# Attention and two feed-forward layers in one kernel: the second phase as a list that the kernel orders itself, silu and gate in one ScalarE step, additions kept in PSUM

## The chip, the cores and the metric

The kernel runs on one core of one Trainium2 chip. The metric is the time of one execution on the device in microseconds (us). The kernel before takes 1124.02 us (median of 3 runs, 1121.6 to 1125.26).

## The reference

The inputs are 4 batches with 8 heads of 576 positions and a head dimension of 64, and 2304 tokens of width 512 go through two feed-forward layers.

```python
scores = scale * (q @ k.T)                      # causal
attn = softmax(scores + minimum(bias, 0))       # bias from cumsum(maximum(s, 0))
x = (attn @ v) as [2304, 512]

xn = x / sqrt(mean(x * x) + 1e-6) * rms_g       # layer 1
g = xn @ w_gate                                 # 512 x 1536
x = (g / (1 + exp(-g)) * (xn @ w_val)) @ w_out  # silu(g) * val, 1536 x 512

h = x @ w_in                                    # layer 2: 512 x 2048
out = (h / (1 + exp(-1.702 * h))) @ w_out       # gate function, 2048 x 512
```

All weights come as 64-bit floats, all else is float32.

## The kernel before, in words

**Number format.** TensorE works on rounded float32. To keep float32 accuracy every operand is split into a rounded part (hi) and the rest (lo), and each product is three matmuls: hi x hi, hi x lo, lo x hi. So behind every intermediate result stand two small steps: `rnd` (a copy on ScalarE, L97) writes hi, `rest` (`scalar_tensor_tensor` on VectorE, L112) writes lo.

**Weights.** They arrive as 64-bit words in units of 128 x 512 (512 KB) by SP's queue. `decode` (L132) makes float32 of one unit: a step on ScalarE (L144), VectorE (L145), GpSimd (L146), VectorE (L147, L149) and GpSimd (L151). The result is then split into hi and lo.

**First phase** (L175 to L627). The 32 heads of attention run one after the other as events with times of their own; the first four chunks (of 128 hidden units) of layer 1 for tokens 0 to 1727 run between them. At its end stand the mean square of the last batch (`rms_mean`, L470 to L480: a root by 12 small steps on 128 x 5 elements on VectorE) and the norm (`rms_apply`, L496).

**Second phase** (`phase_b`, L630). It computes the rest of layer 1 and all of layer 2. The tokens form three blocks p = 0, 1, 2 of 768, each seen as two halves of 384. A list `jobs` (L761) gives the sequence: job P (chunk 4 on block 0), two jobs R (the four first chunks for the remaining 576 tokens, 288 each), ten jobs of layer 1 with chunks 5 to 11 and the rest of 4, twelve jobs of layer 2. A job of the last two kinds has one to three groups and then its outputs.

A *group* (`start_group` L871, `group` L878) is a fast 2 x 2 block product: seven products instead of eight, each of 6 matmuls of 384 columns (`mul`, L858). On the side of the tokens it needs seven *pieces* of the block's input (B11, T1, T2, B22, T3, B21, T4; `MAKE`, L800), each 128 x 2 x 2 x 384 hi and lo, 768 KB; on the side of the weights quarter blocks and four sums of them (S1 to S4, in `front`). There are 23 groups in layer 1 and 24 in layer 2. Its steps off TensorE: three copies out of PSUM on ScalarE (into B, m5 and v1), two additions on VectorE (L889, L896), then `hidden` (L839): tanh on ScalarE (L842) into SBUF and `(tanh + 1) * x` on VectorE (L843); in layer 1 `times` (L854) multiplies this by the other half (L855); then `split_h` (L848) makes hi and lo. That is two hidden blocks in a group of layer 1, four in layer 2.

The *outputs* of a job (`down_part`, L913) are matmuls from the hidden blocks: 384 columns in layer 1 (L922), 512 in layer 2 (L919), 288 in job R; `evac` (L925) adds them to `xT` in SBUF or copies them out.

**Buffers.** PSUM has eight banks: A 2, B 2, E 1, y 3 (L638 to L641). Seven rotating tiles `pc` hold the pieces in use. Two tiles `mk` serve to make pieces *ahead*: while other jobs run, the three blocks' pieces are cut into `mk` and stored in DRAM (`put`, L787, called by way of `pieces`, L803), and at a change of job each of the seven pieces is loaded when the last group of the old job has read its own (`load_piece`, L821).

**What sets the order.** The framework's scheduler places every instruction by priority, which follows the order of the program text; the text itself interleaves the work of later jobs by tables: how many weight units a job decodes (`WPLAN`, L769) and how many pieces it makes ahead (`XSEQ`, `XPLAN`, L771), spread over a job by the class `Spread` (L971). Each engine then executes its queue strictly in that order.

```python
XSEQ = [("1", 2), ("1", 0), ("2", 2), ("2", 1), ("2", 0)]
XPLAN = {2: 3, 3: 4, 5: 7, 11: 4, 12: 5, 13: 5, 14: 7}
...
th = ew.tile([P, H2], F32, tag="th", name="th", bufs=PRM["THB"])[:, :n]
nc.scalar.activation(out=th, in_=src, func=AF.Tanh, scale=0.5 if up is not None else 0.851)
nc.vector.scalar_tensor_tensor(out=th, in0=th, scalar=1.0, in1=src, op0=ALU.add, op1=ALU.mult)
```

## Time and profile before

| | |
|---|---|
| median of 3 runs | 1124.02 us (1121.6 to 1125.26) |
| profiled execution | 1132.93 us |
| its span | 1131.1 us |
| instructions | 17737 |
| mean granted TensorE clock, of full speed | 0.968 |
| HBM read, written | 145.06 MB, 44.26 MB |
| second phase on TensorE | 363.9 to 1127.3 us |

Busy time counts an engine's compute instructions; issuing a transfer or waiting is not in it. "PE" is TensorE's matmuls, "PEld" its weight loads, which run beside them. The span is divided below into stages of the second phase: 363.9 to 395 us (job P and the end of the norm), 395 to 440 (jobs R), 440 to 500 (first groups of layer 1), 500 to 640, 640 to 800 (the change of layers lies in it), and 800 to the end (layer 2). The granted clock is a share of full speed. In a row of idle time, the name behind "<-" is what the engine waited for last.

### The profile page before, as it was taken

What the parts mean: (1) busy time and instruction counts of PE and PEld (TensorE: products, weight loads), DVE (VectorE), ACT (ScalarE), POOL (GpSimd) and SP (SyncE); (2) the same over time, 40 slices, a digit from 0 to 9 for tenths busy, and PEclk for the clock granted to TensorE, in tenths of its full rate; (3) what the DMA queues carried; (4) which work ended last, traced back from release to release, by engine and by line L of the source; (5) the groups of instructions that cost most, each with busy time, mean ns of one, the idle gap of its engine ahead of it and who ended that gap; (6) DMA issues with size and microseconds to landing.
All of it is one profiled execution on the core that took longest, in us unless ns stands there. A gap on an engine that the chain in (4) does not pass through costs nothing.

```text
span 1131.1 us, 17737 instructions
## 1 busy us (share of the span) xinstructions
PE 1057.9 (94%) x6200; PEld 982.0 (87%) x6200; DVE 785.6 (69%) x1625; ACT 574.0 (51%) x1338; POOL 572.0 (51%) x608
## 2 busy tenths in 40 slices
PE   7998999998999698699999999888999999999998
PEld 5776898998999698598999999887888899898987
DVE  6668678678766878585775687986567587556443
ACT  5675677678555445334433445455555344333331
POOL 6788768377832756453640565663265166042000
PEclk9998899999899898798999999999999999999999
DMA  5445424144102477945274258978946516522651
GB/s 151 125 128 141 131 75 125 56 119 124 34 20 75 152 276 276 388 188 218 84 242 164 70 184 327 326 288 308 325 160 221 205 57 217 207 98 70 214 209 66
DMA packets 64511, 193.58 MB, mean 171 GB/s; under 512 B 7091, under 2 KB 26035, under 8 KB 64422
## 3 DMA queue, kind: packets, MB, share of 16 engines
q1 hardware_dynamic: 64310, 192.37, 49.6%
q8 instruction: 49, 0.80, 0.3%
q14 instruction: 40, 0.33, 0.1%
q10 hardware_dynamic: 112, 0.08, 0.0%
HBM read 145.06 MB, written 44.26 MB: 167 GB/s over the span
## 4 chain that ended last, share of the span: by engine, by line
PE 42%; DVE 6%; DMA 5%; ACT 2%; issue 2%; POOL 2%; POOLq 0%; DVEq 0%; ACTq 0%
PE y L919 15%; PE B L863 9%; PE y L922 6%; PE A L863 6%; PE E L863 6%; DMA wst<-in_w_dram 2%; DVE th L843 1%; DVE hh L112 1%; DMA pc<-pc21T 1%; POOL wa L151 1%; DMA pc22B<-mk 1%; ACT th L842 1%; DMA pc<-pc11T 1%; DVE wm L145 1%; DVE wa L149 1%
## 5 line engine op out<-in xcount | busy, mean ns | idle before, releaser
L919 PE MATMUL y<-wu,hh 128*128 128x512 f32 x864 | 213.5, 393 | 6.3 <-ACT hh L97 2.7
L919 PEld LDWEIGHTS y<-wu,hh 128*128 128x128 f32 x864 | 160.4, 188 | 38.9 <-ACT hh L97 4.7
L863 PE MATMUL B<-pc,wu 128*128 128x384 f32 x846 | 172.7, 339 | 6.3 <-ACT th L842 2.8
L863 PEld LDWEIGHTS B<-pc,wu 128*128 128x128 f32 x846 | 151.6, 191 | 10.1 <-ACT th L842 3.1
L112 DVE SCALAR_TENSOR_TENSOR hh<-th,hh 128x384 fp32r<-128x384 f32 (+3 forms) x180 | 128.2, 725 | 39.2 <-ACT hh L97 37.4
L863 PE MATMUL A<-pc,wu 128*128 128x384 f32 x600 | 130.8, 345 | 16.2 <-DVE th L843 13.7
L922 PE MATMUL y<-hh,wu 128*128 128x384 f32 (+1 forms) x672 | 128.1, 331 | 2.3 <-DVE hh L112 1.2
L863 PEld LDWEIGHTS A<-pc,wu 128*128 128x128 f32 x600 | 109.6, 194 | 21.5 <-DVE th L843 15.3
L863 PE MATMUL E<-pc,wu 128*128 128x384 f32 x576 | 121.6, 342 | 4.9 <-DVE xT L496 2.6
L97 ACT ACTIVATE hh<-th 128x384 fp32r<-128x384 f32 (+3 forms) x173 | 84.9, 502 | 69.3 <-DVE th L855 39.1
L922 PEld LDWEIGHTS y<-hh,wu 128*128 128x128 f32 x672 | 115.6, 190 | 3.5 <-DVE hh L112 1.5
L151 POOL TENSOR_TENSOR wa<-wa,wst 128x512 int32<-128x512 int32 x52 | 74.2, 1426 | 77.3 <-DVE wa L149 73.5
L863 PEld LDWEIGHTS E<-pc,wu 128*128 128x128 f32 x576 | 104.8, 193 | 7.3 <-issue 2.9
L687 POOL TENSOR_TENSOR wu<-wa,wu 128x512 fp32r<-128x512 f32 x39 | 54.9, 1408 | 98.9 <-ACT wu L97 98.7
L362 POOL TENSOR_SCALAR p<-p,RC 128x64 f32<-128x64 f32 (+4 forms) x160 | 90.4, 585 | 24.9 <-DVE RC L350 19.5
L166 PE MATMUL gv<-x,wu 128*128 128x256 f32 (+1 forms) x672 | 98.5, 294 | 0.9 <-DVE xT L496 0.9
L338 ACT ACTIVATE p<-p,MX 128x64 f32<-128x64 f32 (+4 forms) x160 | 88.4, 555 | 21.0 <-DVE MX L328 20.5
L166 PEld LDWEIGHTS gv<-x,wu 128*128 128x128 f32 x672 | 90.3, 199 | 1.7 <-issue 1.1
L144 ACT ACTIVATE wst<-wst 128x512 int32<-128x512 uint32 x68 | 46.0, 677 | 86.4 <-DMA wst<-in_w_dram 84.8
L328 DVE CUSTOM_DVE_ANT_0 p<-s,mask 128x64 f32<-128x64 f32 (+4 forms) x160 | 64.7, 422 | 23.8 <-PE s L315 10.9
L382 PE MATMUL t<-ident,p 128*128 128x128 f32 x448 | 74.8, 279 | 4.2 <-ACT pt L103 3.4
L146 POOL TENSOR_SCALAR wm<-wm 128x512 f32<-128x512 f32 x68 | 48.1, 707 | 48.7 <-DVE wm L145 47.5
(141 smaller groups left out, 2076.0 us busy)
## 6 DMA issues: line engine op xcount, KB each, us to landing
wst<-in_w_dram SPq DMA_DIRECT2D x68, 512.0 KB
pc<-pc21T SPq DMA_DIRECT2D x16, 768.0 KB
pc<-pc22T SPq DMA_DIRECT2D x12, 768.0 KB
pc<-pc21B SPq DMA_DIRECT2D x12, 768.0 KB
QS<-in_qT_dram SPq DMA_DIRECT2D x53, 144.0 KB
KS<-in_kT_dram SPq DMA_DIRECT2D x53, 144.0 KB
pc<-pc22B SPq DMA_DIRECT2D x9, 768.0 KB
pc<-pc12T SPq DMA_DIRECT2D x8, 768.0 KB
```

The lines of the kernel that those rows point to most:

```text
L97: nc.scalar.activation(out=o, in_=i, func=AF.Copy, scale=c)
L112: eng.scalar_tensor_tensor(out=o, in0=i, scalar=c, in1=hi, op0=ALU.mult, op1=ALU.subtract)
L151: nc.gpsimd.tensor_tensor(out=ai, in0=ai, in1=li, op=ALU.add)
L166: nc.tensor.matmul(o, w[:, a, wc:wc + P], x(b, k), start=first and n == 0, stop=last and n == 2,)
L328: nc.vector.tensor_tensor_reduce(out=pt[:m, k0:k0 + n], in0=ps[:m, c0:c0 + n], in1=mask[:m, moff:moff + n], scale=-0.125, scalar=mx[:, 4:5 ...
L338: nc.scalar.activation(out=d["p", qb][:m, :], in_=d["p", qb][:m, :], func=AF.Exp, scale=-1.0, bias=MXt[h % NB][:m, col:col + 1], accum_out ...
L362: eng.tensor_scalar(out=pt[:m, :], in0=pt[:m, :], scalar1=RCt[h % NB][:m, qb:qb + 1], scalar2=1.0, op0=ALU.mult, op1=ALU.mult,)
L382: nc.tensor.transpose(ps[:, c:c + m], d["p", qb][:, Q0[kb]:Q0[kb] + P], ident)
L687: lo.tensor_tensor(out=dst[:, 1, :n], in0=src, in1=dst[:, 0, :n], op=ALU.subtract)
L863: nc.tensor.matmul(o[:, :H2], u[:, a, off + k * P:off + k * P + P], pc[:, b, k, :], start=first and k == 0 and m == 0, stop=fin and k == 1 ...
L919: nc.tensor.matmul(ps, hh[c, t][:, a, q * P:q * P + P], wu[layer, c, "o"][:, b, :], start=st, stop=sp_)
L922: nc.tensor.matmul(ps[:, :n], wu["1", c, "o"][:, a, q * P:q * P + P], hh[c, t][:, b, :n], start=st, stop=sp_)
```

## The change

**One list.** `phase_b` no longer issues instructions. Each step is recorded by `op` (L691 of the new kernel) with its engine, its length in us, and the names that it reads and writes; a step marked "VG" may run on VectorE or GpSimd. From the names the dependences follow. A list scheduler then goes through time with these lengths: it keeps an earliest and a latest start of each step, lets VectorE and GpSimd exclude each other in steps marked `port`, models one DMA queue, gives each engine, of what can run, the step with the earliest latest start, and holds an engine back for a short while if a more urgent step is about to be ready. TensorE's own order is that of the text. The result is fixed by dependences between neighbours on each engine. Steps whose start falls before `ET` = 6 us of the phase are issued with priorities among the last events of the first phase; `close_heads` gives back some of that phase's buffers earlier for it.

**Activation.** Silu in layer 1 and the gate function in layer 2 are one ScalarE instruction each (`AF.Silu`, `AF.Gelu_apprx_sigmoid`) in place of tanh, addition and product. In layer 1 it writes `SG` in SBUF, and the product with the other half is written back to PSUM; in layer 2 it works in place. The additions of the group's products are in PSUM too (m5 in layer 2 excepted), and hi and lo are cut from there by a copy and a subtraction.

**Buffers.** Each piece has one fixed tile, six PSUM banks (`FB`) are given out in turn, and two (`BB`) belong to the groups alternately.

**Pieces.** Nothing is made ahead. At a change of job `piece` loads a piece that is in DRAM, or makes it in its tile from `xT` and stores it. The first three products of the next job stand among the last group and the outputs of the old one.

Diff, cut to its core:

```diff
-        XSEQ = [("1", 2), ("1", 0), ("2", 2), ("2", 1), ("2", 0)]
-        XPLAN = {2: 3, 3: 4, 5: 7, 11: 4, 12: 5, 13: 5, 14: 7}
...
-            th = ew.tile([P, H2], F32, tag="th", name="th", bufs=PRM["THB"])[:, :n]
-            nc.scalar.activation(out=th, in_=src, func=AF.Tanh, scale=0.5 if up is not None else 0.851)
-            nc.vector.scalar_tensor_tensor(out=th, in0=th, scalar=1.0, in1=src, op0=ALU.add, op1=ALU.mult)
...
+    def close_heads():
+        pr.close()
+        fs["br"] = ctx.enter_context(tc.tile_pool(name="br", bufs=1, side="right", reuse_waits="tile"))
...
+        def sub(o_, x, y, n, r, w):
+            op("VG", (0.04 + n * 0.00118, 0.1 + n * 0.0025),
+               lambda e: e.tensor_tensor(out=o_, in0=x, in1=y, op=ALU.subtract), r, w, port=True)
+
+        def cp(o_, i_, cost, r, w, t0=-99.0):
+            op("A", cost, lambda e: e.activation(out=o_, in_=i_, func=AF.Copy, scale=1.0), r, w, t0=t0)
...
+        def piece(layer, p, nm):
+
+            key = (layer, p, nm)
+            if key in made:
+                dma(flat(PC[nm]), pc_d[key], 6 << 17, [("pd",) + key], [("pc", nm), ("pc", nm, "lo")])
+                return
+            made.add(key)
+            o, ab = next((o, ab) for x, o, ab in MAKE if x == nm)
+            k, t = BL[o]
+            if ab:
+                (ka, ta), (kb, tb) = BL[ab[0]], BL[ab[1]]
+                sub(xv(k, p, t), xv(ka, p, ta), xv(kb, p, tb), 2 * H2, [xk(ka, p, ta), xk(kb, p, tb)], [xk(k, p, t)])
+            cut(PC[nm], ("pc", nm), xv(k, p, t), xk(k, p, t))
+            dma(pc_d[key], flat(PC[nm]), 6 << 17, [("pc", nm), ("pc", nm, "lo")], [("pd",) + key])
...
+        def split_h(key, src, sk, n, psum):
+            s = new_hh()
+            t = HH[s]
+            cp(t[:, 0, :n], src, 0.17 + n * 0.0008 if psum else 0.53, [sk], [("hh", s)])
+            if psum:
+                op("V", 0.03 + n * 0.00136, lambda e: e.tensor_tensor(out=t[:, 1, :n], in0=src, in1=t[:, 0, :n], op=ALU.subtract),
+                   [sk, ("hh", s)], [("hh", s, "lo")])
...
+        def act(o_, i_, func, n, r, w):
+            op("A", 0.17 + n * 0.0008, lambda e: e.activation(out=o_, in_=i_, func=func), r, w)
+
+        def add(o_, x, y, n, r, w, o=ALU.add):
+            op("V", 0.03 + n * 0.00136, lambda e: e.tensor_tensor(out=o_, in0=x, in1=y, op=o), r, w)
+
+        def gate(bt, bk, n):
+
+            i = sg_i[0] % 2
+            sg_i[0] += 1
+            act(SG[i][:, :n], bt[:, :n], AF.Silu, n, [bk], [("sg", i)])
+            return i
+
+        def gated(key, i, bt, bk, n):
+
+            add(bt[:, :n], SG[i][:, :n], bt[:, :n], n, [("sg", i)], [bk], ALU.mult)
+            split_h(key, bt[:, :n], bk, n, True)
...
+            def m3(self):
+                E, ek = FB[self.E], ("F", self.E)
+                mul(ek, E, self.w["S4"], "B22", False, True)
+                add(E[:, :H2], E[:, :H2], V1, H2, ["v1"], [ek])
+                if self.layer == "1":
+                    self.g1 = gate(E, ek, H2)
+                else:
+                    act(E[:, :H2], E[:, :H2], AF.Gelu_apprx_sigmoid, H2, [], [ek])
+                    split_h((2 * self.c, 1), E[:, :H2], ek, H2, True)
+                    done(self.E)
+
+            def m7(self):
+                E, ek = FB[self.E], ("F", self.E)
+                mul(self.bk, self.bt, self.w["S3"], "T3", False, True)
+                m5, mk_ = M5[self.mi], ("m5", self.mi)
+                if self.layer == "1":
+                    add(E[:, :H2], self.bt[:, :H2], m5, H2, [self.bk, mk_], [ek])
+                    gated((self.c, 1), self.g1, E, ek, H2)
+                    done(self.E)
+                else:
+                    add(m5, self.bt[:, :H2], m5, H2, [self.bk], [mk_])
+                    act(m5, m5, AF.Gelu_apprx_sigmoid, H2, [], [mk_])
+                    split_h((2 * self.c + 1, 1), m5, mk_, H2, False)
...
+            for x, c in enumerate(cs):
+                g = nxt
+                final = x == len(cs) - 1
+                nxt = new_group(job, x + 1) if not final else new_group(after, 0) if after else None
+                pc = (lambda *nms: [piece(*after[:2], nm) for nm in nms]) if final and change else (lambda *nms: None)
+                pc("B11", "T1")
+                g.m3()
+                pc("B22", "T2")
+                if nxt:
+                    nxt.m1()
+                g.m2()
+                g.m7()
+                pc("T3", "B21")
+                if not final:
+                    nxt.m5()
+                    nxt.m6()
+                    g.m4()
+                else:
+                    if len(cs) > 1:
+                        for d in downs[:3]:
+                            d.part(chunks[:-1] if layer == "1" else chunks[:-2])
+                    elif nxt:
+                        nxt.m5()
+                    g.m4()
+                    pc("T4")
+                    if nxt:
...
+                for i in ready[e]:
+                    if start[i] is not None:
+                        continue
+                    o = ops[i]
+                    t = max(free[e], rdy[i], port[0] if o["port"] else -99.0)
+                    c = o["cost"][o["eng"].index(e)]
+                    if t <= tnow and (pick is None or (alap[i], i) < (alap[pick[1]], pick[1])):
+                        pick = (t, i, c)
+                t, i, c = pick
+                o = ops[i]
...
+            if start[i] < PRM["ET"]:
+                key = PRM["EK"] + start[i] / PRM["EU"]
+                with tc.high_priority(offset=tc.cur_priority - round((key + 20.0) * 400)):
+                    ops[i]["fn"](EN[chosen[i]])
+            else:
+                ops[i]["fn"](EN[chosen[i]])
```

The counts by the two orders of instructions: SP's queue has 105 loads of a piece before and 70 now, and 42 writes of one in both. ScalarE loads its function table once before; now it does so three times, ahead of the attention's exponentials, ahead of the first silu and ahead of the first gate function. VectorE has 1625 and 1588 instructions, GpSimd 606 and 494, ScalarE 1180 and 1183; TensorE's 6018 matmuls are the same in number, and its order is the same up to row 351. From GpSimd to VectorE go 51 subtractions that cut lo of weights and 50 sums of quarter blocks.

**ScalarE, end of the second job R and the first group of layer 1.** `y` and `F0` to `F5` are PSUM banks, `re` and `m5` in the first rows take a result on its way to DRAM, `wu` is a weight tile, `wst` a unit being decoded, `th` the tanh, `sg` the silu. Before:

```order
L97 ACTIVATE mk_6375<-xT_70 128x768
L928 ACTIVATE re_5831<-y_5818 128x288
L97 ACTIVATE wu_6029<-ws_6022 128x512
L97 ACTIVATE mk_6444<-xT_70 128x768
L97 ACTIVATE wu_6030<-wm_6023 128x512
L97 ACTIVATE wu_6031<-wb_5968 128x256
L144 ACTIVATE wst_5976<-wst_5976 128x512
L97 ACTIVATE wu_6067<-wa_6057 128x512
L842 ACTIVATE th_5899<-v1_5858 128x384
L842 ACTIVATE th_5919<-A_5834 128x384
```

Now:

```order
L731 ACTIVATE re_5131<-F2_5140 128x288
L731 ACTIVATE B0_5144<-F5_5143 128x384
L731 ACTIVATE m51_5129<-F3_5141 128x288
L731 ACTIVATE m50_5128<-F0_5138 128x384
L731 ACTIVATE wu_1080<-wa_5134 128x512
L731 ACTIVATE v1_5130<-B0_5144 128x384
L731 ACTIVATE re_5131<-F4_5142 128x288
L731 ACTIVATE m51_5129<-F1_5139 128x288
L767 ACTIVATE wst_1294<-wst_1294 128x512
L942 ACTIVATE sg0_5132<-F0_5138 128x384
L731 ACTIVATE B1_5145<-F2_5140 128x384
```

The two copies into `mk` are gone, there are fewer splits of weights, and between the last copies of job R stand the copies into B0, m5 and v1 of the first group.

**TensorE, a change of job in layer 2.** `pc_9934` and `pc_10520` (before) and `pcB11` (now) hold piece B11 of the old and the new block. Before, the old tile is last read in row 2381, 19 rows ahead of the first of these, and the new one first in the last of them:

```order
L863 MATMUL B_10522<-pc_10018,wu_10391 128x384 x6
L919 MATMUL y_10623<-wu_9998,hh_10534 128x512 x3
L919 MATMUL y_10623<-wu_10276,hh_10547 128x512 x3
L863 MATMUL A_10513<-pc_10065,wu_10390 128x384 x6
L919 MATMUL y_10701<-wu_9998,hh_10534 128x512 x3
L919 MATMUL y_10701<-wu_10276,hh_10547 128x512 x3
L919 MATMUL y_10708<-wu_9998,hh_10534 128x512 x3
L863 MATMUL E_10584<-pc_10035,wu_10392 128x384 x6
L863 MATMUL B_10522<-pc_10050,wu_10392 128x384 x6
L919 MATMUL y_10708<-wu_10276,hh_10547 128x512 x3
L863 MATMUL A_10778<-pc_10520,wu_9915 128x384 x6
```

Now (the first row reads the old block's B11, the last the new one's):

```order
L916 MATMUL F4_5142<-pcB11_5111,wu_907 128x384 x6
L916 MATMUL F1_5139<-pcB21_5116,wu_776 128x384 x6
L916 MATMUL B1_5145<-pcT3_5115,w2_5106 128x384 x6
L916 MATMUL F2_5140<-pcT1_5112,wu_1080 128x384 x6
L916 MATMUL B0_5144<-pcT2_5113,wu_1080 128x384 x6
L916 MATMUL B1_5145<-pcT4_5117,w0_5104 128x384 x6
L916 MATMUL F2_5140<-pcB22_5114,wu_1190 128x384 x6
L916 MATMUL F0_5138<-pcB11_5111,wu_776 128x384 x6
```

Between the last reading of the old piece and the first of the new one there stood 28 rows, products and parts of outputs; now there stand six products.

**VectorE, the hand-over between the phases.** `ms` and `ry` belong to the root of the mean square, `pc` are cuts of pieces, `wu`, `wb`, `wm` and `ws` belong to weights, `xT` is the normed input. Before:

```order
L473 TENSOR_SCALAR ms_4973<-ms_4973 128x5
L687 TENSOR_TENSOR wu_5175<-wa_5165,wu_5175 128x512
L475 TENSOR_SCALAR ms_4973<-ms_4973 128x5
L112 SCALAR_TENSOR_TENSOR pc_5191<-xT_70,pc_5191 128x768
L476 TENSOR_SCALAR ry_4979<-ms_4973 128x5
L112 SCALAR_TENSOR_TENSOR pc_5195<-xT_70,pc_5195 128x768
L478 TENSOR_TENSOR ms_4973<-ms_4973,ry_4979 128x5
L112 SCALAR_TENSOR_TENSOR pc_5199<-xT_70,pc_5199 128x768
L479 SCALAR_TENSOR_TENSOR ms_4973<-ms_4973,ry_4979 128x5
L112 SCALAR_TENSOR_TENSOR pc_5202<-xT_70,pc_5202 128x768
```

Now:

```order
L480 TENSOR_TENSOR ms_4981<-ms_4981,ry_4987 128x5
L481 SCALAR_TENSOR_TENSOR ms_4981<-ms_4981,ry_4987 128x5
L482 SCALAR_TENSOR_TENSOR ry_4987<-ms_4981,ry_4987 128x5
L498 SCALAR_TENSOR_TENSOR xT_70<-xT_70,g_sb_78,rb_5006 128x320 x4
L498 SCALAR_TENSOR_TENSOR xT_70<-xT_70,g_sb_78,rb_5017 128x256 x4
L728 TENSOR_TENSOR pcT1_5112<-xT_70,pcT1_5112 128x768
L772 TENSOR_SCALAR wm_5135<-wm_5135 128x512
L728 TENSOR_TENSOR pcB22_5114<-xT_70,pcB22_5114 128x768
L775 SCALAR_TENSOR_TENSOR ws_5110<-wst_1294,wm_5135 128x512
L728 TENSOR_TENSOR pcB11_5111<-xT_70,pcB11_5111 128x768
```

Before, every second row is a cut of a piece or a weight; now the small steps follow each other without anything between them (nine more of them stand ahead of these rows), and the norm comes right behind.

## Rows read from the trace of the kernel before

**Rows 1.** The page: busy time of each engine, share of the span, instructions.

```profile
PE 1057.9 (94%) x6200; PEld 982.0 (87%) x6200; DVE 785.6 (69%) x1625; ACT 574.0 (51%) x1338; POOL 572.0 (51%) x608
```

**Rows 2.** Stages: length; busy PE, PEld, DVE, ACT, POOL; granted clock; DMA share; GB/s.

```profile
363.90:395.00 31.10, 21.26 (x116) 19.87 (x115) 27.10 (x44) 14.75 (x25) 22.67 (x15) 0.84 0.44 159
395.00:440.00 45.00, 40.33 (x268) 39.87 (x268) 33.42 (x52) 19.63 (x38) 26.88 (x22) 0.89 0.73 269
440.00:500.00 60.00, 48.84 (x272) 48.23 (x271) 42.74 (x67) 25.34 (x51) 32.19 (x29) 0.89 0.84 318
500.00:640.00 140.00, 134.81 (x757) 133.59 (x756) 91.99 (x162) 53.55 (x111) 55.89 (x55) 0.98 0.46 160
640.00:800.00 160.00, 147.28 (x791) 139.09 (x789) 128.64 (x190) 77.74 (x152) 91.78 (x74) 0.99 0.77 275
800.00:1127.30 327.30, 325.19 (x1610) 290.35 (x1608) 195.43 (x323) 136.05 (x289) 98.35 (x91) 1.00 0.47 167
sum 763.40, PE 717.71 PEld 671.00 DVE 519.33 ACT 327.06 POOL 327.76; mean PE 119.62 PEld 111.83 DVE 86.55 ACT 54.51 POOL 54.63
```

**Rows 3.** The chain that ended last: start, length, what.

```profile
570.33 4.68 PE y L922 x27
...
618.23 5.55 DMA pc<-pc12B
...
774.77 10.90 DMA pc<-pc21T
...
806.89 8.20 PE y L919 x36
```

**Rows 4.** Timeline of PE: start, length, what; idle time before it in brackets.

```profile
411.64 3.72 PE L922 MATMUL y<-hh,wu 128*128 128x288 f32 x27
...
467.35 2.29 PE L863 MATMUL A<-pc,wu 128*128 128x384 f32 x6 [11.16 <-DVE th L843]
```

**Rows 5.** Waits of PE, 363.9 to 1127: us in total, times, longest.

```profile
PE A L863 <- DVE th L843: 13.7, 5, 11.2
PE E L166 <- DVE th L843: 4.7, 1, 4.7
PE A L166 <- DVE th L843: 4.3, 1, 4.3
...
PE B L863 <- DMA pc<-pc21T: 2.2, 1, 2.2
```

**Rows 6.** Timeline of ACT, 450 to 466 us.

```profile
450.79 0.85 ACT L97 ACTIVATE mk<-xT 128x768 fp32r<-128x768 f32 x1 [1.85 <-DMA pc10T<-mk]
...
464.44 0.63 ACT L97 ACTIVATE wu<-wa 128x512 fp32r<-128x512 f32 x1 [5.50 <-POOL wa L151]
464.98 0.51 ACT L842 ACTIVATE th<-v 128x384 f32<-128x384 f32 x1
```

**Rows 7.** The page: DMA issues, KB each.

```profile
pc<-pc21T SPq DMA_DIRECT2D x16, 768.0 KB
```

**Rows 8.** Groups of VectorE by form: busy us, mean ns, idle us before.

```profile
L112 DVE SCALAR_TENSOR_TENSOR hh<-th,hh 128x384 fp32r<-128x384 f32 x144 | 106.2, 753 | 35.8 <-ACT hh L97 34.3
...
L843 DVE SCALAR_TENSOR_TENSOR th<-th,A 128x384 f32<-128x384 f32 x48 | 26.2, 545 | 4.0 <-ACT th L842 3.8
L889 DVE TENSOR_TENSOR v<-E,v 128x384 f32<-128x384 f32 x47 | 26.0, 553 | 36.2 <-PE E L863 34.7 <-ACT wu L97 1.5
...
L855 DVE TENSOR_TENSOR th<-th,m 128x384 f32<-128x384 f32 x23 | 18.1, 785 | 0.1
```

**Rows 9.** Groups of ScalarE by form.

```profile
L842 ACT ACTIVATE th<-A 128x384 f32<-128x384 f32 x48 | 22.9, 477 | 15.6 <-PE A L863 15.4 <-DVE hh L112 0.2
...
L338 ACT ACT_TABLE_LOAD x1 | 1.3, 1283 | 6.6 <-POOL KB L238 6.6
```

**Rows 10.** Timeline of DVE, 366 to 387 us.

```profile
366.62 0.17 DVE L473 TENSOR_SCALAR ms<-ms 128x5 f32<-128x5 f32 x1
...
375.98 0.16 DVE L480 SCALAR_TENSOR_TENSOR ry<-ms,ry 128x5 f32<-128x5 f32 x1
...
380.90 3.48 DVE L496 SCALAR_TENSOR_TENSOR xT<-xT,g_sb,rb 128x320 f32<-128x320 f32 x8
```

More of the change, by code (lines that the diff above doesn't have):

```diff
@@ L743, in outw @@
             wsub.append((1, o))
+        for c in range(G0):
+            ow["1", c] = 3 * c + 2
         for c in range(G0, NC1):
@@ L819, in phase_b, with cut @@
[L819 to L826 removed]
+        def cut(dst, dk, src, sk, t0=-99.0):
+            cp(dst[:, 0], src, 0.84, [sk], [dk], t0)
+            sub(dst[:, 1], src, dst[:, 0], 2 * H2, [sk, dk], [dk + ("lo",)])
+        made = set()
@@ new lines, in phase_b, with bank, done, mul @@
+        bank_free = list(range(6))
+        def bank():
+            return bank_free.pop(0)
+        def done(b):
+            bank_free.append(b)
+        def mul(bk, bt, w, nm, first, fin):
+            u, off = w
+            wt, pc = WS[u], PC[nm]
+            def fn(e):
+                for k in range(2):
+                    for m, (a, b) in enumerate(((0, 0), (0, 1), (1, 0))):
+                        e.matmul(bt[:, :H2], wt[:, a, off + k * P:off + k * P + P], pc[:, b, k, :],
+                                 start=first and k == 0 and m == 0, stop=fin and k == 1 and m == 2,
+                                 skip_group_check=True)
+            op("T", 1.04, fn, [("w", u), ("w", u, "lo"), ("pc", nm), ("pc", nm, "lo")], [bk])
@@ new lines, in phase_b, with tick @@
+        n = 0
+        for layer, p, cs in jobs:
+            l = "2" if layer == "2" else "1"
+            for c in cs:
+                n += 1
+                last[l, c, "f"] = n
+            n += 1
+            for c in olist(layer, cs):
+                last[l, c, "o"] = n
+        def tick():
+            step[0] += 1
+            declare_w()
+        step[0] = 1
+        declare_w()
+        for t in range(2):
+            mt = MK[t].rearrange("p a k n -> p (a k) n").bitcast(F32)
+            dma(mt, y_d[:, :, t * H2:(t + 1) * H2], 6 << 17, [], [("mk", t)])
@@ new lines, in fn, with new_group @@
+                def fn(e, i=i):
+                    e.matmul(BB[i], WS[2][:, 0, 0:P], WS[2][:, 0, :], start=True, stop=True)
+                op("T", 0.23, fn, [("w", 2)], [("B", i)])
+        ones()
+        tick()
+        for o in [(t, q) for t in range(2) for q in range(KT)]:
+            Down("P", 0, o, [G0], H2).finish(True, False)
+        tick()
+        gi = [0]
+        def new_group(job, x):
+            layer, p, cs = job
+            g = Group(layer, p, cs[x], gi[0])
+            gi[0] += 1
+            return g
@@ new lines, in phase_b @@
+        run_r(0, {})
+        nxt = new_group(SJ[0], 0)
+        run_r(1, {0: (nxt.m1,), 1: (nxt.m5,), 2: (nxt.m6,)})
+        seen = set()
+        for j, job in enumerate(SJ):
+            layer, p, cs = job
+            after = SJ[j + 1] if j + 1 < len(SJ) else None
+            change = after is not None and after[:2] != job[:2]
+            chunks = olist(layer, cs)
+            outs = [3, 4, 5, 0, 1, 2] if layer == "2" else [(t, q) for t in (1, 0) for q in range(KT)]
+            downs = [Down(layer, p, o, chunks, H2) for o in outs]
@@ new lines, in phase_b, with length @@
+            for x, d in enumerate(downs):
+                d.finish(cs[0] == 0, cs[-1] == NC2 // 2 - 1)
+                if x == 2 and nxt and len(cs) > 1:
+                    nxt.m6()
+            tick()
+        N = len(ops)
+        T = 0.0
+        ideal = {}
+        for o in ops:
+            if o["eng"] == "T":
+                ideal[o["i"]] = T
+                T += o["cost"][0]
+        def length(o):
+            return 2.2 + o["byts"] / 360e3 if o["byts"] else min(o["cost"])
+        alap = [1e9] * N
```

816 lines of the change are left out of this document (434 added, 382 removed).

## Prediction, made before the changed kernel had run

> **What bounds the kernel now.** I read the page's busy line first: TensorE is busy 94% of a span of 1131.1 us [rows 1], so it is the bound, and the question is how much of its time is not work. The profiled execution took 1132.9 us; the median of the three runs is 1124.0, 8.9 less. I make the sum against 1132.9 and carry the 8.9 over at the end.
>
> The second phase begins on TensorE at 363.9 us and its last matmul ends at 1127.3. The table by stretches covers these 763.4 us in six stages [rows 2]. Window minus TensorE's busy time gives what it waits: 9.8, 4.7, 11.2, 5.2, 12.7 and 2.1 us, in all 45.7. So the waits lie in four stages before 800 us; behind it the second layer runs almost closed.
>
> The waits are not all that is lost. In full flow a 384-column matmul takes 4.68/27 = 0.173 us, a 512-column one 8.20/36 = 0.228 [rows 3], a 288-column one at most 3.72/27 = 0.138 [rows 4]. The phase has 2598, 864 and 288 of them, and 46 small ones of the first phase stand among them (5 us): 450.2 + 196.8 + 39.7 + 5 = 691.7 us. 763.4 less 691.7 is 71.7 us lost: 45.7 of waiting and 26.0 of slow matmuls. These come right after a wait: behind the longest one, of 11.16 us, six matmuls take 2.29 us instead of 1.04 [rows 4], and the granted clock is 0.84 to 0.89 in the three stretches that wait most and 1.00 in the last [rows 2]. I take a microsecond of waiting to cost 1.57 (71.7/45.7). By stage that is 15.4, 7.3, 17.5, 8.1, 20.0 and 3.3 us.
>
> **Who is late.** TensorE's waits name VectorE's and ScalarE's steps between a product and the hidden block, seldom a transfer [rows 5]. Neither engine is full: VectorE is busy 519 of 763 us. The long wait shows why they are late all the same [rows 6]. ScalarE's queue first waits 1.85 us to refill a buffer that is still being written to DRAM, later 5.50 us for a weight tile that GpSimd has not decoded, and only then runs the tanh on which VectorE, the banks and TensorE hang. Work that nobody needs yet stands ahead of work that TensorE needs.
>
> **The change, part by part.**
>
> *Order.* All second-phase work becomes a list in which each engine takes, of what can run, what is due first. The piece of ScalarE's order in the section above shows it: the two copies into `mk` ahead of the tanh are gone, because pieces are now made at the change of job, straight into the tile that will be used. That empties the mechanism of stages 2 and 3, and most of 5, where the copies of the second layer's pieces stand.
>
> *Transfers.* The order of SyncE has 70 loads of a piece where it had 105, each of 768 KB [rows 7]; writes stay at 42. That is 35 x 0.79 = 27.5 MB less, mostly in the stages in which the DMA engines are busy 73 to 84% [rows 2].
>
> *Activation in one step.* A group in layer 1 goes from 8 VectorE operations to 6, in layer 2 from 10 to 6. Those with an input in PSUM take 0.545 to 0.553 us, those with SBUF alone 0.753 and 0.785 for the same 384 columns [rows 8]; almost all that remain are of the first kind. Layer 1: 4 x 0.55 + 4 x 0.75 = 5.2 us becomes 3.3; layer 2: 6.7 becomes 3.5. Over 23 and 24 groups 121 us of VectorE work go. Against it, 51 more halves of weights and 50 sums of quarter blocks move from GpSimd to VectorE: at 0.73 to 1.4 us and 0.37 to 0.75 us (0.55 scaled by width; twice that when GpSimd is in the way) 56 to 109 us. VectorE's load stays about as it is, off the path; what the step gains is one hop less between product and hidden block.
>
> *ScalarE* keeps its seven operations in a layer-1 group and eleven in a layer-2 group. No row shows silu or gelu. The tanh of 384 columns from PSUM takes 0.477 us [rows 9]; I take 0.48. They could cost less, down to nothing beyond the copy they replace; at 0.7 us, 152 of them would add 33 us to an engine that is busy 327 of 763 us [rows 2], which is cover enough.
>
> *Tables.* The order has three loads of ScalarE's table where it had one; one takes 1.283 us [rows 9]. The load ahead of the first silu lies on the path of the first job: +1.3. The one at the change of layers stands between the last copies of layer 1 and products still to come, where ScalarE is idle about half of the time: nothing; without that cover another 1.3. The Trainium skill, "ScalarE: Activation LUTs", section "What ACT_TABLE_LOAD costs", counts about 1.38 us of drain with each load, 2.66 in all; by it the sum below would be 1.4 us higher. The row has the 1.283 us alone, and no row here shows a switch.
>
> *Hand-over, stage 1.* The mean square is there at 366.6 us, but the last of the 12 small steps of the root is issued at 375.98, with cuts of pieces and weights between them, and the norm is applied from 380.90 on [rows 10]. In the new order the 12 stand in a row (about 0.2 us each, 2.4 us instead of 9.4), and only two pieces are needed before the first matmuls. What comes late next is this first job's own chain: behind the norm (3.48 us) VectorE has three cuts of pieces (about 1 us each), two decode steps, and one product and one half (0.55 each) before the first hidden block, some 8.5 us against 48 x 0.173 = 8.3 us of matmuls; the second hidden block and the split of the remaining tokens come about 3 us behind. I leave 3.8 us of waiting, 6 us lost, of 15.4.
>
> *Later stages.* Six banks in turn take the place of two A, one E and three y, so a late read of one bank no longer stops the next product: of stage 2 I leave 1 us, of stage 3 2, of stage 4 2, of stage 5 3.5, of stage 6 all 3.3.
>
> **The sum.** Left: 6 + 1 + 2 + 2 + 3.5 + 3.3 = 17.8 of 71.7, so 53.9 go and 1.3 comes: 1132.9 - 52.6 = 1080.3 for such an execution, less 8.9: **1071 us**. If nothing at all were lost it would be 1053.6. The first phase is left alone but for its last piece; as its order differs from TensorE's row 351 on, I allow 5 us to either side.
>
> **Rivals.**
>
> *Pieces come too late (slower).* Each piece has one tile. At a change of job the new B11 can be loaded only when the old one has been read for the last time, and in the new order of TensorE six products stand between the two: 6 x 6 x 0.173 = 6.2 us, where 28 rows of products and parts of outputs stood before. Loads on the chain took 5.55 and 10.90 us [rows 3]. There are ten such changes with loads (70/7). At 5.55 nothing is lost; at 10.90 each loses 4.7 x 1.57 = 7.4 us, and ten make 74: 1071 + 74 = 1145. The point from which it decides is a load of 9.6 us, where ten losses eat the gain of 53. Against it: the 10.90 lies where the DMA engines are busy 77% and pieces are both written and read [rows 2], and that doubling is what goes. Chance 0.10.
>
> *Half stays.* The lists are fixed, and an engine that stands waits with all that is behind it. If VectorE's operations in SBUF are stretched beside GpSimd as now [rows 8], or the slow matmuls have another cause than the waits, half of the 53 stays: 1097, from 1086 to 1112. Chance 0.16.
>
> *No difference.* TensorE's work is the same 691.7 us, and if the waits only move (to the weights, whose decoding keeps its length), the time stays at 1124. Against it: GpSimd is busy 328 of 763 us, and the second half of the phase, with as much decoding, hardly waits. Chance 0.04.
>
> *All goes.* Under 1054, with a shorter first phase: 0.04.
>
> **Numbers.** My forecast, 1056 to 1086, has 0.66. Runs of this kernel can tell 0.3%, some 3 us, from no change. Faster: 0.66 + 0.16 + 0.04 = 0.86; same 0.04; slower 0.10. The range from 1052 to 1104 takes in the forecast's own, the case that all goes nearly to its end, and two thirds of the half case, some 0.8.
>
> **What would show it.** In the new profile TensorE's busy share should be 97% or more of the span; the wait of 11 us and both of over 4 us in stages 1 and 2 gone; no wait of ScalarE for a buffer on its way to DRAM; 70 loads of pieces; silu and gelu near 0.48 us; the first phase ending as before. It would be wrong if TensorE waited at each change of job for the first piece, if ScalarE or VectorE now were the ones with no idle time, or if the granted clock stayed under 0.9 where there is no wait.

## The result, and the profile after

The changed kernel takes 1083.32 us (median of 4 runs, 1078.12 to 1085.29) against 1124.21 before: a ratio of 0.9632 with a 95% interval of 0.9593 to 0.9672, or 40.9 us less. Faster was right; 1071 was 12 us too low, and the result lies inside the range of 1052 to 1104. The profiled execution took 1081.84 us, its span is 1079.7 and its mean granted clock 0.990.

The page's busy line, for [rows 1]:

```profile
PE 1040.4 (96%) x6200; PEld 968.9 (90%) x6200; DVE 714.2 (66%) x1588; ACT 581.7 (54%) x1343; POOL 448.3 (42%) x496
```

The second phase by stretches, for [rows 2]: length; busy PE, PEld, DVE, ACT, POOL; granted clock; DMA share; GB/s. The cuts lie where the same work begins: the end of the first job, the first group of layer 1, and the point behind which nothing is lost.

```profile
363.90:389.00 25.10, 21.63 (x123) 19.72 (x121) 18.55 (x41) 11.83 (x20) 8.22 (x5) 0.93 0.47 163
389.00:425.00 36.00, 35.33 (x268) 35.25 (x268) 27.54 (x52) 16.52 (x35) 11.55 (x9) 1.00 0.51 178
425.00:470.00 45.00, 39.87 (x223) 38.90 (x222) 33.59 (x59) 24.61 (x48) 21.02 (x16) 0.97 0.61 216
470.00:1076.10 606.10, 605.96 (x3191) 568.51 (x3189) 362.96 (x639) 278.32 (x563) 161.84 (x139) 1.00 0.50 181
sum 712.20, PE 702.79 PEld 662.38 DVE 442.65 ACT 331.28 POOL 202.63; mean PE 175.70 PEld 165.60 DVE 110.66 ACT 82.82 POOL 50.66
```

763.4 us became 712.2. Of 45.7 us of waiting 9.4 are left (712.20 less 702.79), and from 470 us to the end TensorE is idle for 0.14 us. The clock follows: 1.00 where there were 0.98 and 0.99, and 0.93 and 0.97 in the two stretches that still wait.

TensorE's waits from 330 us on (total, times, longest), for [rows 5]:

```profile
PE F L916 <- ACT m L731: 2.9, 1, 2.9
PE B L916 <- DVE pcT L728: 1.8, 1, 1.8
PE F L1050 <- POOL w L728: 1.7, 1, 1.7
PE o L548 <- DVE yo L105: 1.2, 1, 1.2
PE F L166 <- DVE pcT L728: 0.7, 1, 0.7
```

The waits of 11.2, 4.7 and 4.3 us are gone, and TensorE itself waits for no transfer. The longest one left is a new one. Two timelines show it, ScalarE's and TensorE's near 440 us:

```profile
440.65 0.49 ACT L731 ACTIVATE m<-F 128x384 f32<-128x384 f32 x1 [1.18 <-DMA r<-m]
```

```profile
441.20 3.41 PE L916 MATMUL F<-pcB,wu 128*128 128x384 f32 x18 [2.85 <-ACT m L731]
```

`m` is m5. The second job R uses m5 to carry an output to DRAM, and the group's copy into m5 waits 1.18 us until that transfer has read it; the next product writes the bank that this copy reads.

The new functions, groups of ScalarE by form (busy us, mean ns, idle us before), for [rows 9]:

```profile
L942 ACT ACTIVATE sg<-F 128x384 f32<-128x384 f32 x48 | 23.5, 490 | 20.9 <-DVE F L945 15.7 <-PE F L916 4.9
L942 ACT ACTIVATE F<-F 128x384 f32<-128x384 f32 x48 | 22.7, 477 | 65.6 <-DVE F L945 62.4 <-PE F L916 2.4
...
L942 ACT ACT_TABLE_LOAD x2 | 2.6, 1283 | 0.0
```

From PSUM silu takes 0.490 us and the gate function 0.477, as I took from the tanh. The first table load in ScalarE's timeline:

```profile
374.98 0.85 ACT L731 ACTIVATE pcB<-xT 128x768 fp32r<-128x768 f32 x1 [0.58 <-PE F L916]
375.85 1.28 ACT L942 ACT_TABLE_LOAD   x1
377.14 0.49 ACT L942 ACTIVATE sg<-F 128x384 f32<-128x384 f32 x1
```

The copy ends at 375.83, the load stands from 375.85 to 377.13, the silu starts at 377.14: the switch takes 1.3 us, and TensorE waits for neither of the two. The Trainium skill, "ScalarE: Activation LUTs", section "What ACT_TABLE_LOAD costs", has 1.38 us of drain beside it; this trace shows none.

### The profile page after: what moved, and what is told of

Its sections match the earlier page's. It is cut to its first block, busy times and chain, and to the rows that moved or that the text cites. A ratio compares the mean times of both kernels' runs of the same rounds, so it can differ in the third digit from the quotient of the medians.

```text
span 1079.7 us, 17428 instructions
## 1 busy us (share of the span) xinstructions
PE 1040.4 (96%) x6200; PEld 968.9 (90%) x6200; DVE 714.2 (66%) x1588; ACT 581.7 (54%) x1343; POOL 448.3 (42%) x496
## 3 DMA queue, kind: packets, MB, share of 16 engines
HBM read 117.54 MB, written 44.26 MB: 150 GB/s over the span
## 4 chain that ended last, share of the span: by engine, by line
PE 86%; DVE 7%; DMA 3%; POOL 1%; issue 1%; ACT 1%; SPq 0%; ACTq 0%; DVEq 0%; POOLq 0%
PE F L1047 18%; PE F L916 18%; PE B L916 13%; PE F L1050 10%; PE gv L166 6%; PE t L384 4%; PE v L432 3%; PE o L548 3%; PE s L314 3%; PE F L166 2%; PE v L443 2%; DVE p L330 1%; PE s L316 1%; PE s L317 1%; POOL p L364 1%
## 5 line engine op out<-in xcount | busy, mean ns | idle before, releaser
L1047 PE MATMUL F<-wu,hh 128*128 128x512 f32 x648 | 157.7, 391 | 0.0
L1047 PEld LDWEIGHTS F<-wu,hh 128*128 128x128 f32 x648 | 121.4, 188 | 25.3
L945 DVE TENSOR_TENSOR xT<-F,xT 128x384 f32<-128x384 f32 (+1 forms) x134 | 80.6, 609 | 91.2 <-PE F L1047 65.0
L916 PE MATMUL B<-pcT,wu 128*128 128x384 f32 x630 | 124.8, 336 | 0.0
L916 PEld LDWEIGHTS B<-pcT,wu 128*128 128x128 f32 x630 | 111.5, 188 | 1.6
L916 PE MATMUL F<-pcB,wu 128*128 128x384 f32 x558 | 106.0, 336 | 2.9 <-ACT m L731 2.9
L916 PEld LDWEIGHTS F<-pcB,wu 128*128 128x128 f32 x558 | 98.1, 188 | 3.8 <-ACT m L731 3.2
L1050 PE MATMUL F<-hh,wu 128*128 128x384 f32 (+1 forms) x384 | 73.1, 332 | 0.6 <-DVE hh L935 0.5
L1050 PEld LDWEIGHTS F<-hh,wu 128*128 128x128 f32 x384 | 65.9, 192 | 1.2 <-DVE hh L935 0.8
L916 PE MATMUL F<-pcB,w 128*128 128x384 f32 x324 | 63.5, 338 | 0.0
```

The costliest lines, as they stand in the source:

```text
L916: e.matmul(bt[:, :H2], wt[:, a, off + k * P:off + k * P + P], pc[:, b, k, :], start=first and k == 0 and m == 0, stop=fin and k == 1 and m ...
L945: op("V", 0.03 + n * 0.00136, lambda e: e.tensor_tensor(out=o_, in0=x, in1=y, op=o), r, w)
L1047: e.matmul(ps, h[:, a, q * P:q * P + P], wt[:, b, :], start=st and m == 0, stop=fin and m == 2)
L1050: e.matmul(ps[:, :n], wt[:, a, q * P:q * P + P], h[:, b, :n], start=st and m == 0, stop=fin and m == 2)
```

## The experiments

Twelve kernels. Ratios are to the kernel before, on the same chip; a difference of 0.01 is 11 us.

| kernel | median us | ratio, 95% interval |
|---|---|---|
| before, silu and gate in one step | 1097.69 | 0.9746 (0.9697 to 0.9795) |
| before, no pieces made ahead | 1110.68 | 0.9869 (0.9814 to 0.9923) |
| before, both of these | 1094.25 | 0.9723 (0.9676 to 0.9770) |
| changed | 1083.32 | 0.9632 (0.9593 to 0.9672) |
| changed, tanh as before | 1083.62 | 0.9628 (0.9598 to 0.9658) |
| changed, no due times | 1090.90 | 0.9680 (0.9632 to 0.9728) |
| changed, tanh and no due times | 1112.04 | 0.9878 (0.9843 to 0.9914) |
| changed, equal lengths | 1104.74 | 0.9795 (0.9762 to 0.9829) |
| changed, loads doubled | 1086.60 | 0.9653 (0.9623 to 0.9683) |
| changed, R outputs by way of mk | 1072.97 | 0.9543 (0.9500 to 0.9587) |
| the same, first steps held | 1074.95 | 0.9530 (0.9492 to 0.9567) |
| the same, held later | 1077.49 | 0.9574 (0.9534 to 0.9615) |

### The kernel before, a second profile

> The kernel before once more, unchanged, for a second profile of it. The first profiled execution took 1132.9 us, 8.9 more than the median of the others. Theory: the 8.9 us lie in the second phase, in matmuls at a lower clock behind the waits, so they are part of the 71.7 us that I called lost there. Then this profile, if it is near 1124, shows the first phase ending again near 364 us, the same waits of TensorE (45.7 us in all, within 3), and the 26 us of slow matmuls smaller by about as much as the time is smaller. Rival: the excess is spread over the whole span, a stretch of 0.8%; then the first phase ends near 361 us and the slow matmuls are as before.

It took 1124.75 us with a span of 1123.0, 8.1 less than in the first profile. The matmuls of the mean square, ahead of the root, mark the end of the first phase. The timeline of TensorE in the first profile, then in the second:

```profile
365.31 1.28 PE L470 MATMUL ms<-inv_f,SQ 128*128 128x2 f32 x10 [0.59 <-DVE th L530]
```

```profile
359.58 1.28 PE L470 MATMUL ms<-inv_f,SQ 128*128 128x2 f32 x10 [0.59 <-DVE th L530]
```

5.7 of the 8.1 us lie ahead of this point, in the same program, and 2.4 behind it. My theory, that the excess is part of the 71.7 us lost in the second phase, falls; nor is it an even stretch, since the second phase shrank by 0.3% and the first by 1.6%. The stretch up to this point in the two profiles (columns as in the table of stretches above):

```profile
0.00:365.31 365.31, 341.03 (x2405) 311.61 (x2405) 266.29 (x796) 247.28 (x677) 244.28 (x326) 0.96 0.35 100
```

```profile
0.00:359.58 359.58, 336.68 (x2404) 307.87 (x2405) 269.37 (x796) 247.71 (x677) 245.62 (x326) 0.98 0.36 102
```

Of the 5.7 us, 4.4 are matmuls that took longer (341.03 against 336.68) at a lower granted clock, and 1.4 are waiting. So the lower clock of my theory was there, but in the first phase. In the five profiles of kernels with the first phase of before the clock of this stretch is 0.96 where the point lies at 364.4 and 365.3 us, and 0.97 or 0.98 where it lies at 358.6 to 359.8 (mean of the five 361.5). In the seven with that of the changed kernel the point lies at 360.8 us (clock 0.99) to 366.7 (0.97), mean 363.7. Why the clock differs between executions of one program no run shows.

### Silu and gate function alone

```diff
-            nc.scalar.activation(out=th, in_=src, func=AF.Tanh, scale=0.5 if up is not None else 0.851)
-            nc.vector.scalar_tensor_tensor(out=th, in0=th, scalar=1.0, in1=src, op0=ALU.add, op1=ALU.mult)
+            nc.scalar.activation(out=th, in_=src, func=AF.Silu if up is not None else AF.Gelu_apprx_sigmoid)
```

The 0.5 in `split_h` becomes 1.

> The kernel before with one part of the change alone: silu and gate function as one ScalarE step, its order, pieces and banks as they were. Theory (the order of the queues is what costs): one hop of 0.54 to 0.73 us less in each chain, which shortens the waits a little: 5 to 15 us less than before, 1109 to 1119, and the wait of 11 us stays over 8, since the copies and weights ahead of the activation stand where they stood. Rival (VectorE's activation steps are what costs): most of the gain, 25 to 40 us, so 1084 to 1099. Both: three table loads of 1.28 us, at most 4 us in all.

27.1 us less: the rival's number. The wait of 11 us is gone, at the same product (timeline of TensorE):

```profile
451.76 1.34 PE L862 MATMUL A<-pc,wu 128*128 128x384 f32 x6 [0.83 <-ACT th L842]
```

The activation there came at 450.82 us instead of 464.98 [rows 6]. Between the copy of v1 and the activation ScalarE had two copies into `mk`, five splits of weights and one decode step in its queue before; now it has one copy into `mk`, one cut of a piece and one split. So at this place the framework, too, puts less between the steps of a group when the group has fewer of them, and a step of 0.6 us on VectorE, which I had put off the path, is worth two thirds of the whole gain as long as nothing else is mended. How much of the 27 us is the shorter chain and how much the other order that the framework makes of it was not taken apart.

### Nothing made ahead

```diff
-        XPLAN = {2: 3, 3: 4, 5: 7, 11: 4, 12: 5, 13: 5, 14: 7}
+        XPLAN = {}
...
-                    follow[0] = (cs[-1], lambda nm: load_piece(*nxt[:2], nm))
+                    follow[0] = (cs[-1], lambda nm: change_piece(*nxt[:2], nm))
```

`change_piece` loads a piece that is in DRAM, or makes it in its `pc` tile and stores it.

> The kernel before with another part alone: no pieces made ahead, each piece made at the change of job in the tile that is used (35 loads fewer), order otherwise by the framework's priorities. Theory (copies that nobody needs yet stand ahead of needed work): the wait of 11 us and ScalarE's wait for a buffer on its way to DRAM are gone, 10 to 25 us less than before, 1099 to 1114. Rival (seven cuts of about 0.85 us on ScalarE and 1 us on VectorE in a burst at the change are worse without an order by due times): new waits at the changes for pieces, no gain or up to 20 us slower, 1124 to 1144.

14.1 us less, inside the theory's range. The wait of 11.2 us for VectorE's activation step is at most 3.4 now, but the one in job R grew from 4.7 to 6.3 (waits of TensorE from 363.9 us on):

```profile
PE A L879 <- DVE th L859: 6.6, 5, 3.4
PE E L166 <- DVE th L859: 6.3, 1, 6.3
```

ScalarE's waits to refill `mk` are gone, as the theory had it; one of 3.0 us for the transfer `r<-re` stands ahead of an activation.

### Both parts at once

> The kernel before with both parts at once: silu and gate function in one step, and no pieces made ahead; order by the framework's priorities as before. Alone they gave 27.1 and 14.1 us, in sum 41.2, as much as the whole change (40.9). Theory (both shorten the same waits: in the wait of 11 us, activation, copies made ahead and weights stand in one queue): less than the sum, 28 to 36 us, so 1089 to 1097. Rival (the parts act at different places and add up): 41 us, 1081 to 1086, and the list would add nothing to them.

32.5 us, inside the theory's range: less than the sum of 41.2, and by the ratios no more than silu alone (0.9723 and 0.9746, intervals overlapping). The gains do not add up, as for two parts that shorten the same waits.

### The changed kernel with tanh, without due times, and with both

Tanh (`half` is the tanh, `stt` a `scalar_tensor_tensor` on VectorE; in layer 2 likewise):

```diff
-            act(SG[i][:, :n], bt[:, :n], AF.Silu, n, [bk], [("sg", i)])
+            half(SG[i][:, :n], bt[:, :n], 0.5, n, [bk], [("sg", i)])
+            stt(SG[i][:, :n], SG[i][:, :n], 1.0, bt[:, :n], ALU.add, n, [bk], [("sg", i)])
```

> The changed kernel with the activation as before: tanh on ScalarE, then (tanh + 1) * x on VectorE with the result in PSUM or SBUF, the factor 0.5 folded into steps that exist; the list orders itself by these lengths. Theory (the order is what counts): 1083 to 1093, a ratio to before of 0.963 to 0.973. Rival (the short activation is what counts): 1105 or more, a ratio over 0.983.

No due times:

```diff
-                    if t <= tnow and (pick is None or (alap[i], i) < (alap[pick[1]], pick[1])):
+                    if t <= tnow and (pick is None or (rdy[i], i) < (rdy[pick[1]], pick[1])):
...
-                if e in "AVG":
+                if False:
```

> The changed kernel, its list without due times: each engine takes, of what can run, what was ready first, and is never held back for a more urgent step; lengths, buffers, pieces and activation as changed. Theory (the order by due times is what removes the waits): 1098 to 1120, with waits of over 2 us on weights and hidden blocks again. Rival (short activation, pieces in place and six banks do it, in any sensible order): 1080 to 1088.

Both edits in one kernel:

> The changed kernel with both the activation as before (tanh, addition and product on VectorE) and the list without due times. Each alone cost little: 1083.6 us with the long activation, 1090.9 without due times. Theory (the order by due times is what makes the long activation free, as the short activation is what makes a plain order bearable): together they cost clearly more than the two apart, 1098 to 1115, ratio 0.975 to 0.99. Rival (fixed tiles, six banks in turn and pieces made in place carry the gain): the two losses add, 1086 to 1094, ratio 0.963 to 0.971.

With the order by due times, tanh costs nothing that can be measured (0.9628 and 0.9632). With the short activation, leaving out the due times costs 0.5%, with overlapping intervals: the rival of that expectation was nearer. Without both, 0.9878: 28 us of the 41 are given back, where the two losses apart add up to some 5. So in this kernel the two are substitutes: either keeps the hidden blocks in time. What is left of the gain without both, 1.2%, is no more than pieces made at the change gave alone (0.9869); the banks, the fixed tiles and TensorE's order were not tried apart. TensorE's waits in that kernel from 355 us on:

```profile
PE F L1066 <- ACT hh L934: 8.8, 2, 4.8
PE B L916 <- POOL pcT L728: 6.7, 3, 3.9
PE F L1066 <- DVE hh L936: 3.5, 2, 2.1
```

Hidden blocks (`hh`) and pieces (`pcT`) are late; in the kernel without due times but with silu the first and third of these rows are missing, and the second has 4.6 us.

### Equal lengths in the list

```diff
+            if eng != "T" and not byts:
+                o["cost"] = (0.6,) * len(eng)
             ops.append(o)
```

> The changed kernel, its list with the length 0.6 us for every step of ScalarE, VectorE and GpSimd in place of the measured 0.4 to 1.95 us; due times and all else as changed. Theory (what stands first is what counts, not how exactly it is placed): 1083 to 1093. Rival (the measured lengths carry it: pieces and decoded weights, the long steps, come too late): 1100 or more.

1104.74, the rival: one length for all costs 0.0163, or 18 us, more than no due times at all. Due times and holds worked out from these lengths put steps at worse places than taking what is ready. TensorE's waits:

```profile
PE F L918 <- ACT m L733: 5.2, 1, 5.2
PE F L1052 <- DVE hh L937: 4.3, 4, 1.9
PE B L918 <- DVE F L947: 3.5, 3, 2.6
```

Which lengths matter (GpSimd's taken as VectorE's, or the long steps taken as short) was not tried apart.

### Loads doubled

```diff
             if key in made:
+                xtra[0] += 1
+                dma(flat(MK[xtra[0] % 2]), pc_d[key], 6 << 17, [("pd",) + key], [("mk", xtra[0] % 2)])
                 dma(flat(PC[nm]), pc_d[key], 6 << 17, [("pd",) + key], [("pc", nm), ("pc", nm, "lo")])
```

> The changed kernel with each of its 70 loads of a piece done twice, first into an idle tile: 55 MB more than the changed kernel and 27 MB more than the kernel before. Nothing is left out. Theory (the transfers that went were hidden anyway; TensorE never waits for a piece in the changed kernel's profile): 1082 to 1089, ratio 0.962 to 0.969. Rival (the changes of job stand or fall with the loads): loads that take 10 us and more, a wait of 4.7 us or more at each of ten changes, 1110 to 1145.

0.9653 against 0.9632, intervals overlapping. HBM reads went from 117.54 to 172.59 MB (145.06 in the kernel before), and TensorE waits 0.6 us for pieces (four rows of its waits):

```profile
PE F L919 <- ACT m L731: 4.7, 1, 4.7
PE F L1053 <- ACT hh L731: 1.1, 1, 1.1
...
PE F L919 <- DMA pcB<-pc11B: 0.4, 1, 0.4
PE F L919 <- DMA pcB<-pc21B: 0.2, 1, 0.2
```

In the changed order even 55 MB more are nearly hidden, and one tile for each piece is enough. The wait for the copy into m5, which stands behind a transfer, grew from 2.9 to 4.7 us, and one of 1.1 us for a hidden block came up. In the kernel before TensorE did wait for loaded pieces, 4.1 us in all; whether these went with the 27.5 MB or with the order is not shown.

### Mending what is left

The first repair (the only one in the second of these three kernels):

```diff
-                    t, tk = ((RE, "re"), (M5[1], ("m5", 1)), (V1, "v1"), (M5[0], ("m5", 0)))[q % (4 if p == 0 else 2)]
-                    cp(t[:, :RN], ps[:, :RN], 0.4, [bk], [tk])
+                    if p:
+                        t, tk = MK[q % 2].rearrange("p a k n -> p (a k) n").bitcast(F32)[:, q // 2, :], ("mkr", q)
+                        cp(t[:, :RN], ps[:, :RN], 0.4, [bk, ("yd", 0)], [tk])
...
```

The hold, where `held` names ScalarE's and VectorE's instruction of the last head behind which the phase may begin:

```diff
-        prev = {}
+        prev = dict(fs["held"])
```

> The changed kernel with two repairs of what its profile still shows. One: the outputs of the second job R leave through the two mk tiles, idle by then, instead of re and m5, so that the copy into m5 no longer waits for a transfer (1.18 us on ScalarE, 2.85 us of TensorE behind it). Two: ScalarE's and VectorE's first steps of the second phase are held behind the last head's reciprocal, which came 3.2 us later than before behind two cuts of pieces. Theory (each wait costs TensorE its length and the slow matmuls behind it): 2.85 x 1.57 = 4.5 us and 2 to 3 us, so 1075 to 1078. Rival (other waits take their place): 1081 to 1084.

> The changed kernel with the first of the two repairs alone: outputs of the second job R leave through the mk tiles. The version with both had a ratio to before of 0.953, the changed kernel 0.963, but in its profile the first phase ended no earlier and TensorE's loss between 340 and 360 us had grown from 2.8 to 4.8 us. Theory (all of the gain is this repair): 1074 to 1080, ratio 0.953 to 0.959, the losses between 420 and 460 us gone, 2.5 to 3 us lost between 340 and 360. Rival (the hold gave half of it): ratio 0.959 to 0.963.

> The first repair, and the hold at a later place: ScalarE's first steps of the second phase stand behind the last head's last copy out of its transposes, VectorE's behind its second subtraction there. Theory (cuts of pieces and weights for the second phase hold up the last head, as the made-ahead copies held up the groups before): TensorE loses under 1.5 us between 340 and 360 us as in the kernel before, and 2 us less than the version with the first repair alone: 1072 to 1077. Rival (the first job then waits for its weights instead): no gain, or up to 4 us slower, with a wait of TensorE on a weight near 375 us.

The first repair gives 0.9543 alone and 0.9530 with the first hold, which is no difference; both intervals lie below that of the changed kernel, so this version beats both kernels. With the repair alone, the two longest waits of TensorE from 330 us on are:

```profile
PE B L916 <- DVE pcT L728: 1.4, 1, 1.4
PE o L548 <- DVE yo L105: 1.2, 1, 1.2
```

From the matmuls of the mean square to the end of the span it needs 710.7 us (1077.4 less 366.7) where the changed kernel needs 715.1 (1079.7 less 364.6): 4.4 us. That this is 2.85 x 1.57 is luck: with the wait of 2.85 us the one for a weight (1.7 us, now 0.2) and parts of others went, so that TensorE's idle time from that point to the end of the span fell by 5.1 us (715.07 less 702.65 of busy time, now 710.73 less 703.39). The other 5 to 6 us between the medians lie in executions without a profile: three of this kernel's four had granted clocks of 0.989 to 0.995, those of the changed kernel 0.981 to 0.990.

The hold gave nothing: in the last 30 us before the mean square TensorE is idle 2.8 us with the first form and 3.1 with the second, 2.5 without (with the second, 2.8 us between 340 and 360, where I had expected under 1.5). In the first form the last head's reciprocal came at 340.85 us instead of 345.71, but a copy out of its transposes then stood behind a weight unit that was still on its way, and TensorE waited 1.86 us for it. In the second form TensorE waited for an activation step of the first phase itself:

```profile
PE gv L166 <- DVE th L536: 2.0, 1, 2.0
```

Both moved the wait by a few steps, as the first rival said; the wait for a weight near 375 us, which the other rival named, did not come.

## Why the prediction was right, and where it was off

**The bound: right; its price: rough.** TensorE's waits fell from 45.7 to 9.4 us, and the matmuls in between ran faster with them. For the profiled execution the sum gave 1080.3; it took 1081.84. The forecast's own range, 1056 to 1086, held the median. By the sum's own measure 20.5 us are still lost (712.2 less 691.7) where I left 17.8: 9.4 of waiting, and 11.1 of the 26.0 us of slow matmuls. So 36.3 us less of waiting came with 51.2 us less lost, 1.41 for one, where I took 1.57; the repair gave 4.4 us for 5.1. Where the slow ones lie shows in part: the granted clock is 0.93 and 0.97 in the two stretches that still wait. The time of the rival in which half stays, 1086 to 1112, did not come, though nearly half of the slow matmuls did stay. Three of the signs that I named failed: TensorE is busy 96% of the span and not 97, ScalarE still waits once for a buffer on its way to DRAM (1.18 us), and the first phase does not end as before.

**By stage: errors that cancelled in part.** I left 6 us lost up to the end of the first job, 3.8 of them waiting, and found 3.5 of waiting there (25.10 less 21.63). In stages 4 to 6, where I left 8.8 us, TensorE waits for 0.14 us; its 864 matmuls of 512 columns and 2327 of 384 from 470 us on make 600 us in full flow, so some 6 of 606.1 us are lost there without a wait, by a cause that no run shows. Stage 3, where I left 2, has 5.1 us of waiting alone (45.00 less 39.87): I had read in the diff which tiles carry the outputs of job R, and did not ask who needs m5 next.

**Hand-over: right in its steps, with a cost that I missed.** The root's steps on VectorE's timeline, for [rows 10]:

```profile
365.95 0.17 DVE L475 TENSOR_SCALAR ms<-ms 128x5 f32<-128x5 f32 x1 [0.58 <-PE ms L472]
...
368.19 0.17 DVE L482 SCALAR_TENSOR_TENSOR ry<-ms,ry 128x5 f32<-128x5 f32 x1
...
372.25 3.49 DVE L498 SCALAR_TENSOR_TENSOR xT<-xT,g_sb,rb 128x320 f32<-128x320 f32 x8 [3.90 <-PE rb L493]
```

2.4 us, as forecast. But "the first phase is left alone but for its last piece" was wrong. The last 30 us before the mean square (columns as in the table of stretches above), in the second profile of before, then in the changed kernel:

```profile
329.58:359.58 30.00, 29.41 (x255) 29.12 (x254) 18.27 (x45) 15.20 (x41) 9.95 (x17) 1.00 0.19 57
```

```profile
334.63:364.63 30.00, 27.54 (x233) 26.65 (x231) 22.25 (x52) 16.45 (x41) 13.32 (x16) 1.00 0.12 36
```

TensorE is idle 2.5 us instead of 0.6, while the other engines are busier: cuts of pieces and weight steps of the second phase now stand among the last head's steps. It repeats: all five profiles with the first phase of before have 29.4 us of TensorE's work in these 30, the seven with that of the changed kernel 27.4 to 27.8.

**The activation: the step that I mis-priced.** I gave it "one hop less" and no microsecond of its own. Alone it brings 27 us, two thirds as much as the whole change; inside the list by due times it brings nothing. What I wrote as one mechanism (order) with some extras is two remedies for the same lateness: in the changed kernel either is enough, and both bring no more than one. That neither engine is full and the order makes them late was right; that a shorter chain makes an order without due times bearable I did not see. VectorE's load, which I took to stay, fell from 519 to 443 us in the second phase: if the 121 us went as counted, what came over from GpSimd cost some 45 (121 less 76), under the 56 to 109 I gave it.

**Tables, transfers, loads of pieces: right.** Table loads of 1.283 us on no path of TensorE (I had charged one), HBM reads down by 27.5 MB, and no wait of TensorE for the load of a piece, so the slower rival had nothing to act on.

**The carry: the step that failed.** I took "less 8.9" from the profiled execution to the median. More than half of the excess of that execution was slower matmuls in its first phase, at a lower granted clock (4.4 of 8.1 us, above); the changed kernel's profiled execution had no such excess, and its median lies 1.5 us above it. The carry says that the change saves as much in a usual execution as against the slow profile of before: 52.6. Between the medians it is 40.9. Behind the mean square's matmuls the gain is 48 to 51 us: before it takes 765.8 and 763.4 us to the end of the span (first and second profile), now 715.1, with tanh 718.0. So the second phase gave what was forecast within 5 us, and 7 to 10 us are lost elsewhere. 1.9 of them are the idle time at the end of the first phase (2.46 against 0.59 us). For the rest only the times and granted clocks of other executions stand (1078 to 1085 us for one kernel at 0.981 to 0.990), and no profile that would place it: this stays open.

## What to carry to other kernels

Where an engine waits for a chain of short steps on queues that are not full, a better order and a shorter chain are two remedies for one thing: price them as alternatives, and try the cheaper first. A list that orders itself is only as good as its lengths: with one length for all steps it did worse than taking whatever was ready. And when one profile is slower than the median, look in which part of the program it is slower, and at which granted clock, before the difference is carried into a forecast.

## What was not expected of the hardware

The first phase of one and the same program took 5.7 us more in one profiled execution than in another, 1.6% of it, at a granted clock of 0.96 instead of 0.98. From PSUM silu and the gate function took 0.475 to 0.490 us for 384 columns, as long as tanh (0.477) and as the copies beside them (0.478 to 0.492). The Trainium skill, "ScalarE: Activation LUTs", section "What ACT_TABLE_LOAD costs", says that every function runs at the same rate; this trace agrees. From SBUF the gate function took 0.525 us, and the copy beside it 0.522.
